# A fused attention, routing and two-expert-layer kernel: where the last exponentials of a pair are summed, and the order of the work in the first pair and around the first expert

## The chip, the cores and the metric

The kernel runs on one core of one Trainium2 chip. The metric is the device time of one execution in microseconds; for the kernel before three executions were timed. PE is the matrix engine (TensorE), PEld its weight loads, DVE the vector engine, ACT the scalar engine, POOL the GpSimd engine, and SP (SPq is its queue) the engine that only issues DMA transfers here.

## The reference

Three layers follow each other. B = 2, H = 8, S = 768, D = 64; there are 1536 tokens of width 512.

```python
# 1: attention, masked to the keys of the query's own cluster (16 clusters per head)
q_assign = argmax(q_n . c_n);  k_assign = argmax(k_n . c_n)
scores = where(q_assign == k_assign, q k^T / 8, -1e9)
scores = scores - max(scores, axis=-1)
attn = exp(scores);  attn = attn / (sum(attn, -1) + 1e-9);  x = attn @ v
# 2: mixture of 8 experts, noisy gate, two experts a token
noisy = x @ w_gate + log1p(exp(x @ w_noise)) * noise
for e in range(8): out[tokens of e] += weight * (relu(x @ w1[e]) @ w2[e])
# 3: soft mixture of 8 experts with 4 slots each: softmax over tokens, relu layer, softmax over slots
```

## The kernel before

Attention works on 8 pairs of heads (p = 0 to 7). Keys are split in 6 blocks of 128 and queries in two halves (qh), so a pair has 12 steps t: `score` (line 366) makes 128 keys by 2 x 384 query scores in PSUM with four matmuls and ACT takes their exponential into a buffer `pt` (line 378, five buffers in turn); `av` (line 381) multiplies it with the values; `add` (line 394) sums the exponentials for the denominators. For p = 6 and 7 the blocks kc = 0, 1, 2 are summed on POOL (line 408, then 411, tile `psa`) and kc = 3, 4, 5 on DVE (tile `psb`); only the last block of (7, 1) is not added. `den` (line 430) sums over keys with eight matmuls for each head pair of each part (line 440), and `xout` (line 449) turns and scales the result.

The maximum of a row is taken first, over scores made once more at lower precision: `munit` (line 320) is one such unit, two or one matmuls and one DVE reduction (lines 334, 339, 344), nine for each (p, qh). `mfin` (line 346) puts the nine together and writes the negative maxima as row 96 of the query operand (for p = 0 through PE and ACT, lines 355 and 357). The scores of a half can't start before that row is there. Cluster masks are extra rows 64 to 95 of the operands: `sims`, `masks`, `first_rows` (pair 0) and `mask_rows` (later pairs, by DMA). `hk`, `hq`, `ak`, `aq` are the high parts of q and k, written by ACT, and `akl`, `aql` the low parts, by POOL (lines 306, 316).

The order is written out by hand and every engine runs its instructions in that order. After a set-up the loop at line 1659 goes through 98 steps, two at a time: units of `pre`, two scores, `mid`, the `av` and the `add` of the two steps before, then `post`. Global step s is pair s // 12, t = s % 12. I call two steps a group by its first step: group 84 holds the first two scores of pair 7. `gap` puts the gate's small instructions (lines 539 to 745) between.

The first expert layer (`MoE1`) starts after group 96, in steps s of one eighth of an expert. Its weights come by DMA (`load_w`, line 934, four buffers `wr`), are split in a high part by ACT and a low part by DVE (`split_hi` line 944, `split_lo` line 951, about 0.5 MB each), and go into `first(s)` (line 1046) and `second(s)` (line 1087). Before, six splits (0 to 5) stand in pair 7 (SP, line 57), and split s + 3 stands in step s from s = 3 on. At s = 8 SP reads the order of the later experts (`load_perm`) and issues `load_x(2)`, the gathered tokens of the third job; `load_w(13)` stands ahead of it.

Of the kernel before, what the change touches and what calls it, by code (L numbers as in the profile page):

```python
# [17 lines left out]
NP = B * H // 2  # L18
# [38 lines left out]
SP = 1, 2, 3, 4, 6, 8  # L57
# [3 lines left out]
B7 = 8  # L61
B2 = 1
TF = (0, 0), (0, 1)
ORD, U1, Z1, R1, Z0 = (1, 1, 1, 0, 1, 0, 1, 1), 3, 8, 4, 2
M2S = 14, 15, 16, 18, 20
# [20 lines left out]
class Attention:  # L86
# [6 lines left out]
    def __init__(self, tc, g, qk, q2, k2, v2, cent, wgn):  # L93
# [16 lines left out]
        self.u1 = 0  # L110
# [7 lines left out]
    def load(self, p):  # L118
        nc, g = self.nc, self.g
        q, k = g.raw[p % 2][:, 0:2, :], g.raw[p % 2][:, 2:4, :]  # L120
        nc.sync.dma_start(q, self.q2[p])
        nc.sync.dma_start(k, self.k2[p])
        self.raws[p] = (q, k)
# [9 lines left out]
    def setup(self):  # L133
# [11 lines left out]
        self.identr = self.AQ[1][:, 1, 1, 256:]  # L145
# [46 lines left out]
    def fixed(self):  # L192

        nc = self.nc
        nc.gpsimd.memset(f32(self.BK[0])[96:97], 1.0)
        nc.gpsimd.memset(f32(self.BK[1])[64:96], 0.0)
        nc.gpsimd.memset(f32(self.BK[1])[96:97], 1.0)

    def setup2(self):
# [5 lines left out]
        for hh in range(2):  # L205
            nc.sync.dma_start(self.iw[64 * hh:64 * hh + 64, :, 128 + 16 * hh:144 + 16 * hh],
                              self.wgn.rearrange("(a h p) n -> h p a n", h=2, p=64)[hh])
        self.sel = g.xp.tile([128, 2, 32], F32, name="sel")
        nc.gpsimd.memset(self.sel, 0.0)
        for hh in range(2):  # L210
            nc.gpsimd.memset(self.sel[:, hh, hh:hh + 1], 1.0)

# [31 lines left out]
    def first_rows(self):  # L244
# [18 lines left out]
        self.hk(0, 1)  # L263
# [56 lines left out]
    def munit(self, p, qh, u):  # L320
# [6 lines left out]
        if p or u % 2:  # L327
# [66 lines left out]
    def add(self, p, t):  # L394
# [5 lines left out]
        if kc == first or (p, t) == (NP - 1, 11):  # L400
            return
# [28 lines left out]
    def den(self, p, qh):  # L430
# [3 lines left out]
        if (p, 6 * qh + 5) in self.ptile:  # L434
            parts.append(self.ptile.pop((p, 6 * qh + 5)))
# [32 lines left out]
class Dispatch:  # L468
# [24 lines left out]
    def setup(self):  # L493
# [4 lines left out]
        nc.sync.dma_start(self.noise, self.noise_in)  # L498
# [12 lines left out]
        dv.tensor_scalar(self.lim[:, 1:, :NREG], self.lim[:, 1:, :NREG], float(LATE - RCAP), None, op0=OP.add)  # L511
# [3 lines left out]
        for n in range(0, NSL // 128, 4):  # L515
            m = min(4, NSL // 128 - n)
            io(self.zm[:, n:n + m, 3], [[128, m]], TRASH, 1)
        nc.sync.dma_start(g.xg[:, DM:].rearrange("(n p) d -> p n d", p=128), self.zm)
        dv.tensor_scalar(self.tri, g.jp, 0.0, None, op0=OP.is_gt)
        dv.memset(self.onesb, 1.0)  # L520
        dv.memset(self.cum[:, 0, :], 0.0)
        nc.gpsimd.tensor_copy(g.x[:, :, DM + 3], self.tok)
# [932 lines left out]
def body(tc, qk, q2, k2, v2, cent, wgn, noise, w12, phi, v12, out):  # L1455
    nc = tc.nc
    with ExitStack() as ctx:
# [45 lines left out]
        g.stk = M1.WR.rearrange("p a b -> p (a b)")[:, :2 * S].rearrange("p (a s) -> p a s", a=2)  # L1503
        A = Attention(tc, g, qk, q2, k2, v2, cent, wgn)
        Dp = Dispatch(tc, g, noise)

        A.setup()
        A.sims(0)
        A.busy(B7)
        A.hk(0, 0)  # L1510
        A.hq(0, 0)
# [8 lines left out]
        for i in range(2):  # L1520
            A.ak(0, i)
            A.akl(0, i)
            if i == 0:
                A.fixed()
        for i in range(2):
            A.aq(0, i)
            A.aql(0, i)
        for u in range(A.MU):
# [6 lines left out]
        todo1 = [lambda i=i: A.masks(1, i) for i in range(5)] + [lambda: A.mask_rows(1)]  # L1535
        for i in ORD:
            if i:
                todo1.pop(0)()
            else:
                A.munit(0, 1, A.u1)  # L1540
                A.u1 += 1
        EARLY = A.u1
        A.setup2()
        Dp.setup()
# [6 lines left out]
        for p in range(-1, NP):  # L1551
            s0 = 12 * p
            if p >= 0 and p + 1 < NP:
# [7 lines left out]
                a, z = (2, 7) if p else (U1, Z1)  # L1561
                for u in range(A.MU):
                    at(pre, s0 + a + 2 * u // 3, A.munit, n, 0, u)
                    at(pre, s0 + 8 + 2 * u // 3, A.munit, n, 1, u)
                at(post, s0 + z, A.mfin, n, 0)
                at(post, s0 + 13, A.mfin, n, 1)
# [274 lines left out]
```

## Time and profile before

| | us |
|---|---|
| median of the 3 runs | 648.34 |
| lowest and highest run | 648.06, 650.31 |
| the profiled execution | 641.98 |
| its span (first to last instruction) | 640.2 |
| PE busy in the span | 612.9 (96%) |
| DVE, ACT, POOL busy | 404.2, 311.2, 278.5 |

The profile lists for every engine when it ran and what ended each wait. A row of the timeline gives start, duration, engine, source line, operation, the tile written and the tiles read, how many were merged (xN), and in brackets the idle time before it and what ended it. A row of the stretches gives the length, the busy time of PE, PEld, DVE, ACT and POOL with their instruction counts, the granted PE clock (1.00 is 2.4 GHz, 0.50 is 1.2 GHz), the DMA share and GB/s.

### The profile page before, as it was taken

To read this page: it belongs to the slowest core of one execution; us is meant where nothing else is said; L and a number is where in the kernel's file an instruction comes from. 1 tells how busy PE (TensorE), PEld (TensorE's weight loads), DVE (VectorE), ACT (ScalarE), POOL (GpSimd) and SP (SyncE) were. 2 spreads that over 40 slices of the span, in tenths; PEclk is the share of its full clock that TensorE was granted. 3 is DMA by queue.
4 is the path that set the end of the run, shared out by engine and by line. 5 is a ranking of instruction groups with operands and counts; after the bars stand their busy time and mean duration, and the time that the engine had idled before them with its cause. 6 is when DMAs were issued, how large, how long until landed. Compare 5 with 4: busy or idle time off the path is not lost. (4 is left out here: it accounts for less than half of the span.)

```text
span 640.2 us, 11046 instructions
## 1 busy us (share of the span) xinstructions
PE 612.9 (96%) x3973; PEld 472.5 (74%) x3973; DVE 404.2 (63%) x856; ACT 311.2 (49%) x444; POOL 278.5 (43%) x268
## 2 busy tenths in 40 slices
PE   7899999999999997998999999999999999988996
PEld 5566666666766666886888888888888988876444
DVE  6777888877777688766555445555454557646633
ACT  5576575756767462345344343443534446533002
POOL 3899675858678850733034132332412403120100
PEclk9599999999999898999999999999999999999999
DMA  8392846728344364696926739889795949978995
GB/s 317 81 269 65 305 133 200 247 66 308 118 136 157 150 176 139 221 227 234 193 98 146 198 138 236 323 253 294 255 298 194 194 161 313 313 259 288 429 384 198
DMA packets 62890, 139.47 MB, mean 218 GB/s; under 512 B 15280, under 2 KB 30832, under 8 KB 60784
## 3 DMA queue, kind: packets, MB, share of 16 engines
q1 hardware_dynamic: 56944, 125.31, 58.8%
q0 software_dynamic: 5888, 13.42, 9.6%
q8 instruction: 32, 0.52, 0.4%
q14 instruction: 26, 0.21, 0.1%
HBM read 108.18 MB, written 28.42 MB: 213 GB/s over the span
## 5 line engine op out<-in xcount | busy, mean ns | idle before, releaser
L1087 PE MATMUL py<-ring,H 128*128 128x512 f32 (+1 forms) x686 | 172.4, 395 | 0.7 <-DVE H L1055 0.7
L951 DVE TENSOR_TENSOR ring<-wr,ring 128x1024 fp32r<-128x1024 f32 (+1 forms) x77 | 97.0, 1261 | 105.1 <-ACT ring L944 102.9
L1087 PEld LDWEIGHTS py<-ring,H 128*128 128x128 f32 (+1 forms) x686 | 123.8, 184 | 27.4 <-DVE H L1055 1.7
L944 ACT ACTIVATE ring<-wr 128x1024 fp32r<-128x1024 f32 x77 | 81.5, 1059 | 93.2 <-PE py L1087 80.7
L378 ACT ACTIVATE pt<-psc 128x768 f32<-128x768 f32 x96 | 77.5, 811 | 74.8 <-PE psc L375 66.8
L1095 POOL DMA_INDIRECT x2acc<-y,mdi x31 | 50.4, 1625 | 103.6 <-ACT y L1120 97.7
L391 PE MATMUL pav<-pt,vt 128*64 128x384 f32 x384 | 73.3, 504 | 0.0
L339 DVE TENSOR_REDUCE mp<-pmx 128x1 f32<-128x512 f32 x96 | 63.0, 675 | 14.2 <-PE pmx L334 13.2
L1052 ACT ACTIVATE H<-ph 128x256 fp32r<-128x256 f32 (+7 forms) x80 | 36.6, 458 | 68.1 <-PE ph L1046 62.0
L1046 PE MATMUL ph<-XS1a,ring 128*128 128x240 f32 (+3 forms) x288 | 67.8, 326 | 0.0
L411 POOL TENSOR_TENSOR psa<-psa,pt 128x768 f32<-128x768 f32 x32 | 61.1, 1910 | 5.4 <-ACT pt L378 3.3
L1046 PE MATMUL ph<-XS0a,ring 128*128 128x432 f32 (+3 forms) x252 | 63.2, 333 | 0.1
L1055 DVE SCALAR_TENSOR_TENSOR H<-ph,H 128x384 fp32r<-128x384 f32 (+2 forms) x120 | 43.4, 389 | 18.9 <-ACT H L1052 18.0
L1046 PEld LDWEIGHTS ph<-XS1a,ring 128*128 128x128 f32 x288 | 47.8, 188 | 3.6 <-DVE ring L951 0.2
L1046 PE MATMUL ph<-XS0b,ring 128*128 128x256 f32 (+3 forms) x192 | 46.7, 316 | 2.6 <-ACT ring L944 2.0
L1046 PE MATMUL ph<-XS1b,ring 128*128 128x240 f32 (+3 forms) x192 | 46.1, 314 | 0.8 <-DVE ring L951 0.8
L1046 PEld LDWEIGHTS ph<-XS0a,ring 128*128 128x128 f32 x252 | 43.6, 191 | 2.7 <-issue 0.6
L1014 POOL TENSOR_TENSOR XS0b<-xr,XS0a 128x512 fp32r<-128x512 f32 (+1 forms) x9 | 16.8, 1871 | 64.7 <-ACT XS0a L1008 64.7
L391 PEld LDWEIGHTS pav<-pt,vt 128*64 128x64 f32 x384 | 23.5, 136 | 24.9 <-issue 19.4
L749 POOL DMA_INDIRECT xg<-x,idx x24 | 26.3, 1096 | 25.4 <-DVE inv L682 19.0
L344 DVE TENSOR_REDUCE mp<-pmx 128x2 f32<-128x512 f32 x48 | 33.0, 690 | 6.1 <-PE pmx L334 6.0
L334 PE MATMUL pmx<-even 96*128 96x512 f32 (+1 forms) x96 | 33.9, 411 | 1.6 <-ACT even L258 0.8
(364 smaller groups left out, 1003.2 us busy)
## 6 DMA issues: line engine op xcount, KB each, us to landing
wr<-in_w SPq DMA_DIRECT2D x80, 512.0 KB
v<-in_v SPq DMA_DIRECT2D x9, 2048.0 KB
xg<-xr SPq DMA_DIRECT2D x14, 512.0 KB
wr<-in_qk SPq DMA_DIRECT2D x8, 768.0 KB
early<-in_q SPq DMA_DIRECT2D x8, 768.0 KB
early<-in_k SPq DMA_DIRECT2D x8, 768.0 KB
x2acc<-xr SPq DMA_DIRECT2D x8, 512.0 KB
vt<-in_v SPq DMA_DIRECT2D x8, 384.0 KB
```

The source lines that it names most:

```text
L334: nc.tensor.matmul(o, self.BQ[i][:96, qh, hh, 128 * c:128 * c + 128], self.BK[i][:96, hh, ks], start=True, stop=True)
L339: nc.vector.tensor_reduce(mp[:, 0, col:col + 1], ps, axis=AX.X, op=OP.max)
L378: nc.scalar.activation(pt, ps[:, :, :384], AF.Exp, scale=SCALE)
L391: nc.tensor.matmul(self.avp[p, qh][64 * hh:64 * hh + 64, :384], self.vt[p][:, hh, kc, :], pt[:, hh, :], start=(kc == 0), stop=(kc == 5))
L411: eng.tensor_tensor(s, s, pt.pop((p, t)), op=OP.add)
L944: self.nc.scalar.activation(self.ring[s][0], self.wr[s], AF.Copy)
L951: nc.vector.tensor_tensor(lo[:, :n], wr[:, :n], f32(hi)[:, :n], op=OP.subtract)
L1046: nc.tensor.matmul(ph[:, :u], a[:, 128 * c:128 * c + 128], x[:, c, :u], start=(c == 0 and i == 0), stop=(c == 3 and i == 2))
L1052: nc.scalar.activation(HH[:, :u], ph[:, :u], AF.Relu)
L1055: nc.vector.scalar_tensor_tensor(o[:, :b - a], ph[:, a:b], 0.0, f32(HH)[:, a:b], op0=OP.max, op1=OP.subtract)
L1087: nc.tensor.matmul(o, x, y, start=(f == 0 and i == 0), stop=(f == NF - 1 and i == 2))
L1095: st = nc.gpsimd.indirect_dma_start(out=out, out_offset=bass.IndirectOffsetOnAxis(ap=di, axis=0), in_=y, in_offset=None, compute_op=OP.add)
```

## The change

Each exponential that DIRECT names (the last block of (6,0), (6,1), (7,0), and the last three of (7,1)) goes into `den` as a part of its own and is not added on DVE. `den` and `xout` of pair 6 come one step earlier. Pair 7 has five splits, spread two steps apart; splits 5 to 8 stand in the expert steps 0 to 3, each with the load of the weight four further on; from step 8 on `load_w` stands behind `load_perm` and `load_x(2)`. In the set-up k is loaded ahead of q for pair 0, `hk(0, 1)` comes right behind `hk(0, 0)`, the gate's constants on POOL come first, and the three memsets of `fixed` come between and behind POOL's low parts. `lim`, `tri`, `onesb`, `cum` and the loads of the noise and of `zm` move to step 31. In group 0 the two scores stand ahead of `masks(1, 3)`, `masks(1, 4)`, `mask_rows(1)` and of three units; the units of pair 1 start in group 4. Three dummy matmuls go (B7).

```diff
-SP = 1, 2, 3, 4, 6, 8
+SP = 1, 3, 5, 7, 9
+DIRECT = {(6, 0): 1, (6, 1): 1, (7, 0): 1, (7, 1): 3}
-B7 = 8
+B7 = 5
+EARLY = 2
-ORD, U1, Z1, R1, Z0 = (1, 1, 1, 0, 1, 0, 1, 1), 3, 8, 4, 2
-M2S = 14, 15, 16, 18, 20
+FIRST = 3 * (4,) + 4 * (6,) + 4 * (8,) + 4 * (10,) + 3 * (12,)
+R1, Z0 = 3, 2
+M2S = 15, 15, 17, 18, 20
...
     def load(self, p):
-        nc.sync.dma_start(q, self.q2[p])
-        nc.sync.dma_start(k, self.k2[p])
+        for t, src in ((k, self.k2), (q, self.q2)) if p == 0 else ((q, self.q2), (k, self.k2)):
+            nc.sync.dma_start(t, src[p])
...
-    def fixed(self):
+    def fixed(self, i):
-        nc.gpsimd.memset(f32(self.BK[0])[96:97], 1.0)
-        nc.gpsimd.memset(f32(self.BK[1])[64:96], 0.0)
-        nc.gpsimd.memset(f32(self.BK[1])[96:97], 1.0)
+        if i:
+            nc.gpsimd.memset(f32(self.BK[1])[64:96], 0.0)
+        nc.gpsimd.memset(f32(self.BK[i])[96:97], 1.0)
...
     def first_rows(self):
-        self.hk(0, 1)
         krows(1)
...
     def munit(self, p, qh, u):
-        if p or u % 2:
+        if p or qh or u % 2:
             ps = g.psum.tile([128, 512], F32, tag="mx", bufs=2, name="pmx")
...
     def add(self, p, t):
-        if kc == first or (p, t) == (NP - 1, 11):
+        if kc == first or kc >= 6 - DIRECT.get((p, qh), 0):
             return
...
     def den(self, p, qh):
-        if (p, 6 * qh + 5) in self.ptile:
-            parts.append(self.ptile.pop((p, 6 * qh + 5)))
+        parts += [self.ptile.pop((p, 6 * qh + kc)) for kc in range(6) if (p, 6 * qh + kc) in self.ptile]
...
         A.setup()
+        A.setup2()
+        Dp.setup()
         A.sims(0)
         A.busy(B7)
         A.hk(0, 0)
+        A.hk(0, 1)
...
         for i in range(2):
             A.ak(0, i)
             A.akl(0, i)
-            if i == 0:
-                A.fixed()
         for i in range(2):
             A.aq(0, i)
+            if i == 0:
+                A.fixed(0)
             A.aql(0, i)
+        A.fixed(1)
...
-        A.setup2()
-        Dp.setup()
+        for i in range(3):
+            A.masks(1, i)
+        for u in range(EARLY):
+            A.munit(0, 1, u)
...
+                for fn in (0, 0, lambda: A.masks(1, 3), lambda: A.masks(1, 4), lambda: A.mask_rows(1)):
+                    at(pre, 0, fn or (lambda: None))
                 for u in range(EARLY, A.MU):
-                    at(pre, (u - EARLY) * 2 // R1, A.munit, 0, 1, u)
+                    at(pre, 0 if u < EARLY + R1 else 2, A.munit, 0, 1, u)
...
-                    for s, fn in zip(LT[qh] if p == NP - 1 else (8, 10, 12), (A.total, A.den, A.xout)):
+                    for s, fn in zip(LT[qh] if p == NP - 1 else (8, 9, 11) if p == NP - 2 else (8, 10, 12), (A.total, A.den, A.xout)):
...
+        at(post, 1, A.load_g)
+        at(post, 31, Dp.setup2)
...
         for s in range(ns):
             j, f = M1.steps[s]
-            if 4 + len(SP) <= s + 5 < ns:
-                M1.load_w(s + 5)
             if s == LX:
                 while todo:
                     gap(1000, 1000)
                 M1.load_perm()
                 M1.load_x(2)
+            if 13 <= s + 5 < ns:
+                M1.load_w(s + 5)
...
-            if len(SP) <= q < ns:
+            if s < 4:
+                q = s + 5
+            if s < 4 or 9 <= q < ns:
                 M1.split_hi(q)
                 M1.split_lo(q)
+            if s < 4:
+                M1.load_w(q + 4)
```

## Rows read from the trace of the kernel before

**Rows 1.** The page: busy time of the engines; the costliest group of splits (busy, mean ns).
```profile
PE 612.9 (96%) x3973; PEld 472.5 (74%) x3973; DVE 404.2 (63%) x856; ACT 311.2 (49%) x444; POOL 278.5 (43%) x268
...
L951 DVE TENSOR_TENSOR ring<-wr,ring 128x1024 fp32r<-128x1024 f32 (+1 forms) x77 | 97.0, 1261 | 105.1 <-ACT ring L944 102.9
```

**Rows 2.** Stretches: length, busy of PE, PEld, DVE, ACT, POOL; clock, DMA share, GB/s.
```profile
120.00:140.00 20.00, 20.00 (x141) 14.21 (x141) 15.25 (x35) 11.15 (x16) 11.94 (x8) 1.00 0.56 183
...
20.00:30.00 10.00, 7.97 (x27) 5.07 (x27) 6.33 (x13) 4.64 (x7) 8.44 (x43) 0.50 0.31 98
...
6.00:8.00 2.00, 1.57 (x10) 0.49 (x11) 0.91 (x7) 0.00 (x0) 0.00 (x0) 1.00 1.02 427
...
30.00:32.00 2.00, 2.00 (x9) 1.96 (x8) 1.01 (x3) 0.53 (x1) 2.00 (x2) 0.64 0.71 44
...
212.00:214.00 2.00, 2.00 (x13) 1.82 (x13) 1.16 (x3) 0.98 (x2) 1.83 (x2) 0.91 0.35 136
...
248.00:250.00 2.00, 2.00 (x10) 2.00 (x10) 1.43 (x8) 0.00 (x0) 0.00 (x0) 0.52 0.01 4
```

**Rows 3.** Timeline, all engines, from the start to the second row of maxima.
```profile
9.08 0.56 DVE L231 TENSOR_TENSOR xr<-xr 128x384 bf16<-128x384 f32 x1
...
9.79 0.84 ACT L295 ACTIVATE even<-early 64x768 fp32r<-64x768 f32 x1 [4.72 <-DMA early<-in_k]
...
10.72 1.83 POOL L306 TENSOR_TENSOR even<-early,even 64x768 fp32r<-64x768 f32 x1 [8.79 <-ACT even L295]
...
18.81 3.90 POOL L316 TENSOR_TENSOR even<-early,even 64x768 fp32r<-64x768 f32 x2
...
19.66 0.80 ACT L357 ACTIVATE even<-pnm 1x768 fp32r<-1x768 f32 x1
19.66 1.38 DVE L231 TENSOR_TENSOR xr<-xr 128x384 bf16<-128x384 f32 x1
...
22.86 0.52 PE L373 MATMUL psc<-even 97*128 97x384 f32 x1
...
25.67 0.69 DVE L511 TENSOR_SCALAR lim<-lim 128x2 f32<-128x2 f32 x1 [2.30 <-POOL lim L510]
...
35.83 0.80 ACT L357 ACTIVATE even<-pnm 1x768 fp32r<-1x768 f32 x1 [0.96 <-PE pnm L355]
```

**Rows 4.** Timelines of DVE, POOL and PE, the end of attention and the first expert.
```profile
204.05 2.42 DVE L411 TENSOR_TENSOR psb<-psb,pt 128x768 f32<-128x768 f32 x1
...
235.03 0.96 DVE L411 TENSOR_TENSOR psb<-psb,pt 128x768 f32<-128x768 f32 x1
...
241.52 1.30 DVE L1001 STREAM_TRANSPOSE xr<-xr 128x512 f32<-128x512 f32 x2
...
257.94 0.42 DVE L1055 SCALAR_TENSOR_TENSOR H<-ph,H 128x256 fp32r<-128x256 f32 x1 [0.40 <-ACT H L1052]
...
228.39 1.85 POOL L411 TENSOR_TENSOR psa<-psa,pt 128x768 f32<-128x768 f32 x1
...
208.10 0.50 PE L334 MATMUL pmx<-oddb 96*128 96x256 f32 x2 [1.43 <-DVE mp L339]
...
236.04 0.54 PE L440 MATMUL pden<-psb,sel 128*32 128x96 f32 x16 [1.02 <-DVE psb L411]
...
246.29 0.74 PE L440 MATMUL pden<-psb,sel 128*32 128x96 f32 x16 [4.10 <-DVE psb L408]
...
258.94 0.19 PE L728 MATMUL prank<-xr,tri 128*128 128x24 bf16 x1 [0.46 <-DVE xr L682]
```

**Rows 5.** Timeline, SP, ACT and PE, expert steps 12 to 14: the weights' DMA and who waits.
```profile
284.37 1.96 SPq L940 DMA_DIRECT2D wr<-in_w  x2
...
290.88 1.06 ACT L944 ACTIVATE ring<-wr 128x1024 fp32r<-128x1024 f32 x1 [4.67 <-DMA wr<-in_w]
...
287.02 1.59 PE L1046 MATMUL ph<-XS0b,ring 128*128 128x256 f32 x12
...
291.99 0.50 PE L1046 MATMUL ph<-XS0b,ring 128*128 128x256 f32 x2 [1.99 <-ACT ring L944]
```

More of the change, by code (lines that the diff above doesn't have):

```diff
@@ L109, in __init__ @@
         self.ptile, self.stile, self.avp, self.ots, self.rds = {}, {}, {}, {}, {}
-        self.u1 = 0
     def busy(self, n):
@@ L143, in setup @@
         half = lambda n: g.place(n // 2).bitcast(BF16)
-        self.identr = self.AQ[1][:, 1, 1, 256:]
+        self.identr = g.turner
         nc.gpsimd.tensor_copy(self.identr, g.ident)
@@ L204, in setup2 @@
             nc.gpsimd.tensor_copy(self.iw[:, hp, :128], g.ident)
-        for hh in range(2):
-            nc.sync.dma_start(self.iw[64 * hh:64 * hh + 64, :, 128 + 16 * hh:144 + 16 * hh],
-                              self.wgn.rearrange("(a h p) n -> h p a n", h=2, p=64)[hh])
         self.sel = g.xp.tile([128, 2, 32], F32, name="sel")
@@ L211, in setup2, with load_g @@
             nc.gpsimd.memset(self.sel[:, hh, hh:hh + 1], 1.0)
+    def load_g(self):
+        for hh in range(2):
+            self.nc.sync.dma_start(self.iw[64 * hh:64 * hh + 64, :, 128 + 16 * hh:144 + 16 * hh],
+                                   self.wgn.rearrange("(a h p) n -> h p a n", h=2, p=64)[hh])
     def sims(self, p):
@@ L497, in setup @@
                                                      allow_small_or_imprecise_dtypes=True)
-        nc.sync.dma_start(self.noise, self.noise_in)
         io(self.iode, [[-1, E]], E, 0)
@@ L510, in setup @@
         nc.gpsimd.tensor_tensor(self.lim, self.base, self.capm[:, None, :].to_broadcast([128, B, E]), op=OP.add)
-        dv.tensor_scalar(self.lim[:, 1:, :NREG], self.lim[:, 1:, :NREG], float(LATE - RCAP), None, op0=OP.add)
         io(self.tok, [[128, NCK]], 0, 1)
@@ L517, in setup, with setup2 @@
             io(self.zm[:, n:n + m, 3], [[128, m]], TRASH, 1)
+        nc.gpsimd.tensor_copy(g.x[:, :, DM + 3], self.tok)
+    def setup2(self):
+        nc, g = self.nc, self.g
+        dv = nc.vector
+        nc.sync.dma_start(self.noise, self.noise_in)
         nc.sync.dma_start(g.xg[:, DM:].rearrange("(n p) d -> p n d", p=128), self.zm)
+        dv.tensor_scalar(self.lim[:, 1:, :NREG], self.lim[:, 1:, :NREG], float(LATE - RCAP), None, op0=OP.add)
         dv.tensor_scalar(self.tri, g.jp, 0.0, None, op0=OP.is_gt)
@@ L521, in setup @@
         dv.memset(self.cum[:, 0, :], 0.0)
-        nc.gpsimd.tensor_copy(g.x[:, :, DM + 3], self.tok)
     def fill(self, i):
@@ L1503, in body @@
         g.stk = M1.WR.rearrange("p a b -> p (a b)")[:, :2 * S].rearrange("p (a s) -> p a s", a=2)
+        g.turner = M1.XT[1][0][:, :128]
         A = Attention(tc, g, qk, q2, k2, v2, cent, wgn)
@@ L1534, in body @@
         turn()
[L1535 to L1542, printed above, removed]
-        A.setup2()
-        Dp.setup()
+        for i in range(3):
+            A.masks(1, i)
+        for u in range(EARLY):
+            A.munit(0, 1, u)
         pre, mid, post = {}, {}, {}
@@ L1560, in body @@
                     at(post, s0 + s, fn, n, i)
[L1561 to L1566, printed above, removed]
+                if p == 0:
+                    at(pre, 4, lambda: None)
+                for u in range(2 * A.MU):
+                    qh, v = divmod(u, A.MU)
+                    at(pre, s0 + (2, 8)[qh] + 2 * v // 3 if p else FIRST[u], A.munit, n, qh, v)
+                for qh in range(2):
+                    at(post, s0 + 7 + 6 * qh if p else (9, 13)[qh], A.mfin, n, qh)
             if p == 0:
+                for fn in (0, 0, lambda: A.masks(1, 3), lambda: A.masks(1, 4), lambda: A.mask_rows(1)):
+                    at(pre, 0, fn or (lambda: None))
                 for u in range(EARLY, A.MU):
-                    at(pre, (u - EARLY) * 2 // R1, A.munit, 0, 1, u)
+                    at(pre, 0 if u < EARLY + R1 else 2, A.munit, 0, 1, u)
                 at(post, Z0, A.mfin, 0, 1)
@@ L1583, in body @@
                 if p + 4 < NP:
-                    at(post, max(s0 + 15, 0), A.load_s, p + 4)
+                    at(post, max(s0 + 15, 3), A.load_s, p + 4)
         for n in range(2, NP):
```

## The prediction

> **What bounds the kernel now.** I read the page first: PE is busy for 612.9 us of a span of 640.2 [rows 1], so 27 us of waiting is all that a better order can take from PE, unless it also takes away slow time. Next the stretches: in the middle of attention PE is busy for all of its 20 us at full clock [rows 2], and nothing that is moved there pays. Two kinds of place are left. From 20 to 30 us PE is busy for 7.97 us of 10 and the granted clock is 0.50, that is 1.2 GHz [rows 2]: the first pair waits and is slow besides. And in the timelines of the end of attention PE stops for 1.43 us at 206.7, 1.02 at 235 and 4.10 at 242, each time for DVE [rows 4], and in the first expert for 1.99 us at 290, for a weight [rows 5]. The clock falls behind two of these: it is 0.91 over 212 to 214 and 0.52 over 248 to 250 [rows 2]. So the change is judged in three stages: the first pair, the end of attention, and expert steps 0 to 14.
>
> **The start.** Before, ACT begins `hk(0,0)` at 9.79 because k lands last [rows 3]. One of the two transfers is 786 KB; at 427 GB/s [rows 2] that is 1.8 us, so with k first `hk` runs from about 8.0 and POOL's L306 from 8.8, where it ran from 10.72 for 1.83 us [rows 3]. But DVE's L231, which all masks of pair 0 wait for, stands at 9.08. Alone it takes 0.56; beside POOL's L316 the same instruction took 1.38 [rows 3], as if it waited for POOL's instruction to end. So L231 would now wait until 10.6 and end at 11.1 instead of 9.64. I take 1.2 us later for the first masks and so for the first maxima (0, if POOL does not hold it, and 1.5). The constants on POOL now run beside DVE's set-up, from 2 to 6.5 us. Their bounds: nothing, or what L511 shows, 0.69 us for two elements beside a POOL memset [rows 3], some 0.5 too much, for each of nine steps, 4.5. I take 0, because POOL's single constants are short beside the memset of L511 and up to 1 us of delay disappears in L231's wait for L306. The Trainium skill, page "SBUF — State Buffer", section "Who interferes with whom", says that a DVE instruction with two SBUF inputs is shut out only by a GpSimd instruction that reads SBUF, and tensor_scalar in its two-port modes by any: by it L306 would hold L231, and of the set-up the four tensor_scalar steps alone could be held, 4 x 0.5 = 2.0 us at most instead of 4.5; L511 in the trace agrees.
>
> **The first pair.** Row 96 of the first half was written by L357 from 19.66 to 20.46; 1.2 later is 21.7. Score 0 began at 22.86 [rows 3], behind a wait for POOL's low parts and for the mask of pair 1. With the memsets behind `aql(0,0)` POOL is done with it by about 16, and the mask matmul now stands behind scores 0 and 1, so score 0 starts at 21.7: 1.2 us won. From there to the second L357 (35.83 [rows 3]): 2.03 us of idle lie in 20 to 30 [rows 2], of which about 0.5 lies behind score 0 and goes. The clock, at 0.64 over 30 to 32, came back at 31.4 [rows 2]; after the restart at 208.10 it came back by 212.4 (0.91 over 212 to 214), 4.3 us later [rows 2, 4]. If PE runs without a gap from 21.7 it comes back near 26; 5.4 us of half clock less is worth 2.7. Two units of pair 1 leave the stretch, 0.2 each. Sum 1.2 + 0.5 + 2.7 + 0.4 = 4.8. DVE must still take nine reductions and POOL its twelve 1.8 us additions and differences, which starts only 2 us earlier, so I take 4.0 us. The low end is 1.5: the clock comes back only after a pause of PE for DVE's third reduction. High end 5.2, without L231's wait. From group 4 on PE was full, so this gain stays.
>
> **Moved out of the start.** The noise, `zm` and four DVE steps (0.69 for L511 [rows 3], 1.6 together) now come at step 31, where DVE is busy 15.25 of 20 and PE 20.00 [rows 2]: cost 0 beside PE; 1.6 if DVE had no room. Three dummy matmuls of PE go where PE waits for L231 anyway: 0. `load_g` behind group 0 is needed by the first `xout` only: 0.
>
> **Direct denominators.** Each adds one part to `den`, 0.54 us for a part [rows 4]; there are four more, 2.0 us on PE at most. In return L411 at 204.05 goes, which took 2.42 us beside POOL, with PE's wait of 1.43 and the 4.3 us at half clock behind it (2.1) [rows 2, 4]; L411 at 235.03 goes with the wait of 1.02; and L408 in front of the wait of 4.10 goes [rows 4]. That would be 8.6 us. It is not all won, for what is late next is known: exponential 91 needs the buffer that POOL's L411 frees at 230.24 [rows 4], and POOL runs from 203.8 to there almost without a pause; it gets perhaps 1.5 faster, so PE can be at most some 2.6 us ahead there. Behind it DVE sets the pace: it reaches the transposes of the first tokens at 241.52 without a wait [rows 4]. Of its queue two L411 of 0.96 and one split of 1.26 [rows 1, 4] go, 3.2 us, and splits further apart meet POOL less often. I take the transposes 3.7 us earlier. From there the gate's chain on DVE leads to `second(0)`, and L408, about 0.9, goes from it: 4.5 us earlier in all. PE will then wait for the `ot` of ACT and for DVE's H where it waited for L408; these waits are inside the 4.5. Low end 2.5 (the tokens' DMA, issued when POOL's scatters have landed, gets no earlier), high end 5.4.
>
> **Splits 5 to 8 in steps 0 to 3.** Split 5 now stands between the gate's last exponential and `second(1)`'s H: ACT 1.06 [rows 5], then DVE 1.26 [rows 1], both in front of the H at 257.94 and of the gate steps that the rank matmul at 258.94 waits for; PE had already waited 0.46 for it [rows 4]. 1.06 + 1.26 less the 0.40 that DVE waited there: PE loses 2.0. Splits 6 to 8 come in front of nothing that PE needs within its 2.8 us a step: 0; if each cost as much, 6 more.
>
> **Weight 13 behind the tokens.** `load_x(2)` waits for the experts' order; the first weight behind it went at 284.37 and ACT had it at 290.88 [rows 5]: that was weight 14. Now it is weight 13 that stands there. `first(13)` ran at 287.02 and would start at 291.99, as `first(14)` did; the wait of 1.99 and 0.2 becomes one of 5. PE has one step less done at that time: 2.8 us lost. Bounds: -0.7 (a weight issued at 284.37 lands in 3 us) and 4.9 (the clock falls in a wait of 5 us as it did behind 4.10, 2.1 more).
>
> **Sum.** 4.0 + 4.5 - 2.0 - 2.8 = 3.7 us won. Against the profiled execution (span 640.2, 641.98 with what lies around it) that is 638.3; the median of the three runs is 6.4 us above the profiled one, and I take the same difference from it: 648.34 - 3.7 = 644.6.
>
> **The rivals.** (a) Weight 13 is not late, since the DMA engines take it beside the tokens; for it speaks that the tokens' pieces leave GB/s unused, against it weight 14 in the same place. Then 3.7 + 2.8 = 6.5 won: 641.8. (b) The clock takes the gain: PE pauses in group 0 and it comes back late (1.5 instead of 4.0), or it falls in the 5 us wait (2.1 lost): 1.2 to 1.6 won, 646.9. For it speaks that it fell behind 1.43 us of waiting [rows 2, 4]; against, that it did not behind the 1.99 at 290. (c) Slower: the splits in steps 0 to 3 come in series with the gate on DVE, each at the 2.0 us of split 5. It decides where DVE's work of a step, with H, gate steps and a split, exceeds PE's 2.8 us. Then 4.0 + 4.5 - 8.0 - 2.8 = -2.3, and with the clock falling in these pauses -4.4: 650.6 to 652.7. The single wait of 0.46 speaks against DVE being that full; its 28 gate steps in step 0 speak for it. (d) The direct parts save nothing because POOL's chain holds PE: 2.0 less, 646.6; I count it with (b).
>
> **How the numbers follow.** Forecast 0.40 (643 to 646.2), (a) 0.15, (b) with (d) 0.32, (c) 0.13. About 0.5% or 3.2 us is what a measurement of this kernel can tell from no change. Faster than 645.1: (a) and most of the forecast, 0.48. Slower than 651.6: the dear half of (c) and mishaps, 0.09. The rest, 0.43, is within. For 8 in 10 the range takes (a) and the cheap half of (c): 640.5 to 649.5.
>
> **What would show it.** Score 0 near 21.7, the second L357 near 31.8, clock back near 26; L231 over 1 us long at the start. No L411 of DVE from 200 us on, no PE wait at 206 or 235; a wait for `ot`, not for `psb`, at the last `den`. A PE wait of about 2.5 us in front of the rank matmul, and one near 5 us in front of `first(13)` for weight 13. It is wrong if that last one is missing, if the clock is low for long in group 2, or if `second(2)` to `second(5)` wait for H.

## The result and the profile after

The change made the kernel slower by half a per cent, 3.6 us between the medians, where it was forecast 3.7 us faster; the time is above the range (640.5 to 649.5) too.

| us | before | after |
|---|---|---|
| median (20 executions each) | 648.33 | 651.97 |
| lowest and highest | 643.72, 650.44 | 647.25, 656.21 |
| ratio, 95% interval | | 1.0052 [1.0032, 1.0072] |
| the profiled execution | 641.98 | 647.25 |
| its span | 640.2 | 645.4 |
| PE busy, DVE busy | 612.9, 404.2 | 612.1, 397.1 |

To see where the time went, both traces are cut at starts of PE instructions that stand in both: px(p, qh), the first matmul of `xout` (L459) for pair p and half qh, and `first(s)`. Lines of after are those of before plus 3 to 6 (its L411 is the L408 of before); `lim` and `tri` stand at 525 and 526. (What the recorded texts of the experiments call first(1) and first(3) are first(2) and first(4) here: first(0) and first(1) run as one.) The third column is a second trace of the same changed kernel, the fourth a second trace of the kernel before; both come with the experiments.

| stage, us | before | after | after again | before again | forecast |
|---|---|---|---|---|---|
| start to px(0,0) | 56.80 | 52.18 | 56.77 | 55.34 | 4.0 won |
| to px(1,1) | 39.77 | 39.76 | 39.72 | 39.81 | 0 |
| to px(2,0), with step 31 | 13.76 | 15.65 | 17.01 | 13.79 | 0 |
| to px(5,1) | 93.39 | 93.36 | 93.37 | 93.37 | 0 |
| to first(2), with second(0) | 50.37 | 48.55 | 46.79 | 51.56 | 4.5 won |
| to first(4), with split 5 | 6.43 | 8.31 | 8.28 | 6.16 | 2.0 lost |
| to first(8) | 11.25 | 13.74 | 11.24 | 17.53 | 0 |
| to first(13), with weight 13 | 15.25 | 18.57 | 18.55 | 15.26 | 2.8 lost |
| to first(16) | 13.49 | 13.52 | 12.57 | 13.62 | 0 |
| to the end | 339.67 | 341.78 | 340.44 | 339.17 | 0 |
| sum | 640.18 | 645.42 | 644.74 | 645.61 | 3.7 won |

Four things stand out. Step 31 costs 1.9 to 3.3 us. Weight 13 costs 3.3. The start is worth 4.6 in one execution and nothing in another. And the kernel before itself takes 7.2 us more between px(5,1) and first(8) in its second trace than in its first: 1.2 to first(2) and 6.3 from first(4), less 0.3 between.

**The start**, timeline of the kernel after (start, duration, engine, line, operation), then two stretches (length, busy of PE, PEld, DVE, ACT, POOL; clock, DMA share, GB/s):
```profile
4.98 0.80 DVE L176 TENSOR_SCALAR xr<-xr,cnn 128x64 f32<-128x64 f32 x1
...
9.02 1.77 DVE L235 TENSOR_TENSOR xr<-xr 128x384 bf16<-128x384 f32 x1
...
8.55 3.90 POOL L309 TENSOR_TENSOR even<-early,even 64x768 fp32r<-64x768 f32 x2 [1.85 <-ACT even L298]
...
21.50 0.41 PE L376 MATMUL psc<-even 97*128 97x384 f32 x1 [0.47 <-ACT even L360]
...
20.00:30.00 10.00, 8.98 (x58) 5.88 (x56) 8.77 (x17) 7.82 (x11) 4.71 (x4) 0.99 0.34 111
```
The mask step L235 ends with POOL's first difference, as it was forecast: 1.77 us where L231 took 0.56 [rows 3]. Score 0 starts at 21.50, forecast 21.7, and 20 to 30 us run at a clock of 0.99 instead of 0.50 [rows 2]. The second trace of the same kernel does not have that; the mask step in it, held for longer, and the same stretch:
```profile
8.93 2.07 DVE L235 TENSOR_TENSOR xr<-xr 128x384 bf16<-128x384 f32 x1
...
8.77 3.91 POOL L309 TENSOR_TENSOR even<-early,even 64x768 fp32r<-64x768 f32 x2 [2.09 <-ACT even L298]
...
20.00:30.00 10.00, 9.62 (x36) 6.42 (x36) 6.41 (x11) 4.88 (x7) 3.28 (x3) 0.50 0.28 96
```

**Step 31**, timeline of the kernel after:
```profile
94.10 1.71 DVE L525 TENSOR_SCALAR lim<-lim 128x2 f32<-128x2 f32 x1
95.72 0.21 DVE L526 TENSOR_SCALAR tri<-ident_i 128x128 bf16<-128x128 f32 x1
...
93.96 1.82 POOL L411 TENSOR_TENSOR psa<-pt 128x768 f32<-128x768 f32 x1
...
96.74 0.50 PE L337 MATMUL pmx<-oddb 96*128 96x256 f32 x2 [1.83 <-DVE mp L342]
```
A step of two elements per partition takes 1.71 us, until POOL's sum ends. DVE's next reduction is late by that, and PE waits 1.83 for the bank of the maxima that it frees. In the second trace PE waits 1.82 there, and the clock falls to 0.50 behind it, which makes 17.01 of the stage where the first has 15.65. Timeline of that trace and a stretch behind it:
```profile
101.28 0.56 PE L337 MATMUL pmx<-oddb 96*128 96x256 f32 x2 [1.82 <-DVE mp L342]
...
102.00:104.00 2.00, 2.00 (x8) 0.54 (x6) 2.00 (x2) 0.00 (x0) 1.92 (x2) 0.50 0.29 83
```

**The end of attention and the first expert**, timeline of the kernel after:
```profile
237.81 1.30 DVE L1007 STREAM_TRANSPOSE xr<-xr 128x512 f32<-128x512 f32 x2
...
242.62 1.08 PE L459 MATMUL px<-iw,ot 128*128 128x160 f32 x6 [1.83 <-ACT ot L424]
...
256.22 0.19 PE L734 MATMUL prank<-xr,tri 128*128 128x24 bf16 x1 [2.33 <-DVE xr L688]
...
283.93 1.65 SPq L946 DMA_DIRECT2D wr<-in_w  x3
...
289.02 1.06 ACT L950 ACTIVATE ring<-wr 128x1024 fp32r<-128x1024 f32 x1 [5.90 <-DMA wr<-in_w]
...
290.12 3.23 PE L1052 MATMUL ph<-XS0b,ring 128*128 128x256 f32 x12 [3.22 <-ACT ring L950]
...
280.00:300.00 20.00, 16.78 (x87) 14.60 (x86) 7.87 (x12) 7.56 (x11) 5.32 (x4) 0.83 0.79 219
```
The transposes come at 237.81, 3.7 us before 241.52 [rows 4]; but 2.8 of these were won ahead of px(5,1) (200.95 against 203.72), so the end of attention itself brings them forward by 0.9, and in the second trace by 2.7 (241.94 behind a px(5,1) at 206.87). PE waits for `ot` and no longer for `psb`; the rank matmul waits 2.33 instead of 0.46 for the gate, behind split 5. `first(13)` waits 3.22 for weight 13 and then takes 3.23 us, where it took 1.59 [rows 5]: it runs at 1.2 GHz.

### The profile page after: what moved, and what is told of

It reads as the page before. It is cut to its first block, busy times and chain, and to the rows that moved or that the text cites. A ratio compares the mean times of both kernels' runs of the same rounds, so it can differ in the third digit from the quotient of the medians.

```text
span 645.4 us, 11153 instructions
## 1 busy us (share of the span) xinstructions
PE 612.1 (95%) x4031; PEld 472.2 (73%) x4031; DVE 397.1 (62%) x852; ACT 310.7 (48%) x444; POOL 278.8 (43%) x268
## 5 line engine op out<-in xcount | busy, mean ns | idle before, releaser
L1052 PE MATMUL ph<-XS0b,ring 128*128 128x256 f32 (+3 forms) x192 | 48.2, 327 | 3.6 <-ACT ring L950 3.2
L1052 PEld LDWEIGHTS ph<-XS0b,ring 128*128 128x128 f32 x192 | 32.3, 201 | 6.2 <-ACT ring L950 3.6
```

The costliest lines, as they stand in the source:

```text
L1052: nc.tensor.matmul(ph[:, :u], a[:, 128 * c:128 * c + 128], x[:, c, :u], start=(c == 0 and i == 0), stop=(c == 3 and i == 2))
```

## The experiments

Ratios are to the kernel before on the same chip; as recorded they differ from the ratio of the medians by up to 0.3%. They carry from chip to chip only roughly: the kernel after has 1.0052 in the result and 1.0115 on another chip, which is 4 us. A price that is a difference of two ratios, taken on different chips or at different times, is no surer than that, so the stages of the traces decide where they can. "Lost to the clock" is the span times one less the mean granted clock, averaged over the executions behind the ratio; it tells how much of a difference is slow PE time. For the kernel after it is 15.2 us; for the kernel before 14.2 on the chip of the first four experiments.

### Weight 13 ahead of the tokens

Undoes one move only.
```diff
+            if 13 <= s + 5 < ns:
+                M1.load_w(s + 5)
             if s == LX:
...
                 M1.load_x(2)
-            if 13 <= s + 5 < ns:
-                M1.load_w(s + 5)
```


> The changed kernel with one order put back: in expert step 8 the load of weight 13 is issued ahead of the third expert's tokens. Theory: the place in SP's queue is the whole cause of the wait of 3.22 us in front of first(13) and of the half clock behind it; first(13) then starts without a wait near 286.7 and weight 14 takes over the wait, near 2 us as in the kernel before; 4 us less than the changed kernel, so about 648 us, level with before. Rival: the load is slow because the DMA engines share it with the tokens whatever the order; then first(13) still waits 2 us or more and the time stays at 651 to 652. In both, everything ahead of 280 us is the changed kernel's own: if the results of PE at 206, 223 and 262 us come late again, that belongs to the program; if they don't, it was that one execution.

Measured: 646.38 against 648.67, ratio 0.9968 [0.9944, 0.9992]. Timeline of this kernel, the mask step at the start, `first(13)` and `first(14)`:
```profile
8.87 0.56 DVE L235 TENSOR_TENSOR xr<-xr 128x384 bf16<-128x384 f32 x1
...
8.90 4.02 POOL L309 TENSOR_TENSOR even<-early,even 64x768 fp32r<-64x768 f32 x2 [2.21 <-ACT even L298]
...
285.88 1.59 PE L1052 MATMUL ph<-XS0b,ring 128*128 128x256 f32 x12
...
289.18 0.50 PE L1052 MATMUL ph<-XS0b,ring 128*128 128x256 f32 x2 [0.32 <-ACT ring L950]
```
Both waits are nearly gone, that of weight 14 too, for which the recorded text wanted near 2 us. The stage takes 15.20 us instead of 18.57, the one behind it 11.79 instead of 13.52. In all traces it is 15.2 to 15.3 with weight 13 ahead of the tokens (10 traces) and 18.5 to 20.0 behind them (7). From a ratio of 1.0052 to 0.9968 is 5.4 us; the time lost to the clock falls from 15.2 to 10.5, so 4.7 of the 5.4 are slow PE time. Not all of it need be weight 13's: at the start, where the program is that of the kernel after, DVE came to the mask step 0.03 us ahead of POOL in this execution and was not held, and px(0,0) came at 50.85 instead of 52.18. Weight 13 was late as forecast, and the clock fell in its wait, as the second half of rival (b) said.

### Step 31 without `lim`

`lim` goes back to the set-up, now on POOL.
```diff
-        dv.tensor_scalar(self.lim[:, 1:, :NREG], self.lim[:, 1:, :NREG], float(LATE - RCAP), None, op0=OP.add)
+        nc.gpsimd.tensor_scalar(self.lim[:, 1:, :NREG], ..., float(LATE - RCAP), None, op0=OP.add)   # in setup
```


> The changed kernel with the one-column addition on lim done by POOL in the set-up instead of by DVE at step 31. Theory: DVE stood 1.71 us in lim behind POOL's sum of exponentials, which held PE for 1.83 us and cost 1.9 of the 4.6 us won at the start; without it the gain stays 4.6 to px at 203.7, PE has no wait near 96.7, and the time is 1.9 us less, 650.1. Rival 1: the four instructions at step 31 take DVE's room whatever lim does (0.7 us more work): the wait stays at 1 us or more. Rival 2: the gain is there at 200 us but POOL's and DVE's chain at the end of attention takes it back, 651.5 or more.

Measured: 648.7 against 648.67, ratio 1.0009 [0.9979, 1.0040]. Timeline of this kernel at step 31:
```profile
94.94 1.77 DVE L526 TENSOR_SCALAR tri<-ident_i 128x128 bf16<-128x128 f32 x1
...
94.80 1.82 POOL L411 TENSOR_TENSOR psa<-pt 128x768 f32<-128x768 f32 x1
...
97.51 0.50 PE L337 MATMUL pmx<-oddb 96*128 96x256 f32 x2 [1.76 <-DVE mp L342]
```
The wait only moved: `tri`, 0.21 us in the kernel after, now takes 1.77. It isn't the operand but the place: whichever tensor_scalar comes first there stands behind POOL's sum. So this run didn't mend step 31, and its 2.8 us against after are no price of it.

### Splits back, direct denominators back

Two undo one part each: the splits and loads of weights 4 to 13 as before; and DIRECT reduced to what the kernel before did.
```diff
-SP = 1, 3, 5, 7, 9
+SP = 1, 2, 3, 4, 6, 8
...
-            if s < 4 or 9 <= q < ns:
+            if len(SP) <= q < ns:
```


> The changed kernel with the splits and loads of weights 4 to 13 where the kernel before has them. Theory: the wait in front of the rank matmul goes from 2.33 to about 0.5 and first(13) has no wait: 1.9 + 4.0 = 5.9 us less than the changed kernel, 646.1. Rival 1: splits 5 to 8 in steps 0 to 3 also cause the late H in steps 4 to 7 (second(4) waits 0.75, second(5) 1.22): then 2.5 more goes, 643.6. Rival 2: the gate's chain on DVE paces steps 0 to 2 whatever the splits do: only weight 13's share is won, 648.

```diff
-DIRECT = {(6, 0): 1, (6, 1): 1, (7, 0): 1, (7, 1): 3}
+DIRECT = {(7, 1): 1}
...
-        ... else (8, 9, 11) if p == NP - 2 else (8, 10, 12)
+        ... else (8, 10, 12)
```


> The changed kernel without the direct denominators of pair 6 and of the first half of pair 7, with one direct part in the last half and den and xout of pair 6 at the old steps. Theory A: the direct parts win what the changed trace shows for this stage, 1.8 us up to first(0); without them PE's waits of 1.43 at 206, 1.02 at 235 and 4.10 at 242 are back and the time is 653.8. Theory B, as forecast: they are worth 4.5 us and something else took the rest; then 656.5. Rival: the earlier den of pair 6 is itself what makes PE's results late at 206 and 223; then the time is that of the changed kernel or less, 650 to 652, with no wait of DVE for psc there.

Measured: 647.83, ratio 0.9967 [0.9940, 0.9994]; and 648.97, ratio 0.9991 [0.9958, 1.0023]; both against 648.67. The first is no better than weight 13 alone. The second is a surprise: without the direct denominators the kernel is not slower than the kernel after, but rather faster. In both traces ACT or DVE start on some results of PE late, without a cause among the waits that the profile names, which led to the next runs.

### The kernel before again, and the kernel after without its scatters

> The kernel before, unchanged, in one more profiled execution beside the others on this chip. Theory: the late arrival of PE's results (up to 3 us after the matmul's recorded end, in all five profiles of changed kernels) belongs to the order of the changed program; here none of some 650 results comes more than 0.3 us late, as in the first profile of this kernel. Rival: it belongs to the chip or to the execution; then late results show here as well, near 206 to 229 and 258 to 272 us.

```diff
     def scatter(self, ...):
+        return
```


> The changed kernel without the gate's scatters of the tokens (POOL's indirect DMAs from 203 us on are left out, so the experts get empty rows); all else stands. Theory: PE's late results in 206 to 225 and 258 to 270 us come from POOL's chain of scatters, since every late group lies inside such a chain; then none of PE's results is late by more than 0.3 us here, DVE's first reduction behind den(6,0) follows at once, and second(4) and second(5) don't wait for H. Rival: they come from PE's own stream; then the same 2.5 and 3.0 us stand behind den(6,0) and first(5).

Measured, one execution each: the kernel before has a span of 645.6 in this trace, 5.4 more than in the first (647.39 against a median of 648.75); the kernel after without scatters takes 646.35. Timeline of the kernel before again, `first(4)`, the second layer's matmuls behind, and the activation of the result of `first(4)`:
```profile
260.03 1.53 PE L1046 MATMUL ph<-XS0a,more 128*128 128x256 f32 x12
...
266.86 2.18 PE L1087 MATMUL py<-more,H 128*128 128x512 f32 x6 [2.48 <-issue]
...
266.42 0.38 ACT L1052 ACTIVATE H<-ph 128x256 fp32r<-128x256 f32 x1 [7.74 <-remote]
```
PE ends the first row at 261.56, and ACT, idle for 7.74 us, starts on the result at 266.42, 4.9 us later. The same is to be seen in the kernel after, at 206 us, where POOL's scatters run:
```profile
206.36 0.51 PE L442 MATMUL pden<-pt,sel 128*32 128x96 f32 x16
...
209.45 0.28 DVE L445 STREAM_TRANSPOSE dt<-pden 128x96 f32<-128x96 f32 x1 [4.42 <-PE psc L378]
209.62 1.51 ACT L381 ACTIVATE pt<-psc 128x768 f32<-128x768 f32 x2 [4.79 <-PE psc L378]
...
206.36 1.02 POOL L755 DMA_INDIRECT xg<-x,idx  x1 [0.16 <-issue]
207.68 0.98 POOL L755 DMA_INDIRECT xg<-x,idx  x1 [0.30 <-issue]
```
and not in the kernel without scatters, at the same `den`:
```profile
211.97 0.51 PE L442 MATMUL pden<-pt,sel 128*32 128x96 f32 x16
...
212.55 0.28 DVE L445 STREAM_TRANSPOSE dt<-pden 128x96 f32<-128x96 f32 x1 [1.91 <-PE pden L442]
```
DVE is at the result 0.07 us behind PE's end here, 2.58 in the kernel after. I counted results of PE that DVE or ACT, idle, took up more than 0.3 us after PE's recorded end: 0 of 655 in the first trace of before, 18 in its second, 12 in after, 10 to 17 in the six experiments with scatters on these two chips, 0 without scatters. All lie between 205 and 276 us, while POOL issues scatters or just behind them. That points to the scatters, though on one trace without them. They don't suffice, as the first trace of before shows and the next chip will; and while POOL's 31 later indirect DMAs run, which add the experts' rows, nothing comes late. What is late is PE's signal, the update of its semaphore, which the trace records apart from the matmul's end and mostly 0.01 us behind it. In the kernel after, the updates for ends at 206.87, 207.30, 208.00, 208.24 and 208.94 all stand between 209.42 and 209.61, while PE went on with its next matmuls.

What goes with it is seen from first(4) to first(8): 11.2 to 11.8 us in the six traces in which no result is late by over 0.44 us, 13.7 to 20.5 in the other eleven (17.4 to 20.5 with the old splits, 13.7 to 19.4 with the new ones).

### Only the start, and the start with the direct denominators

Both take `lim` out of step 31 and undo the splits and loads; the first undoes the direct denominators too.

> Of the change only the start and the first pair are kept (with the noise, zm and the small constants at step 31, and lim done by POOL in the set-up); direct denominators, splits, loads and the steps of pair 6 are those of the kernel before. Theory: 4.6 us are won up to px of pair 2 as in the changed kernel and nothing behind that place loses them: 643.7 to 644.5, ratio about 0.993. Rival 1: the end of attention is paced by POOL and DVE and takes the gain back: score 96 moves by less than 2 us and the time stays above 646.5. Rival 2: the late results of PE come with the start's edits; then they show in this trace too, and the time is 646 or more.

> As the kernel that keeps only the start, and with the direct denominators and the earlier den of pair 6 as well. Theory A (as forecast): the direct parts take the transposes 3.7 us and second(0) 4.5 us forward; with nothing behind that loses it, 4.5 us less than the start alone, 639.5. Theory B (the changed trace): PE's results come late behind den(6,0), which leaves 1.8 us: 642. Rival: the direct parts cost more than they save, as the kernel without them suggests (0.9991 of before where the changed kernel stood at 1.0052): this one is 1 to 4 us slower than the start alone.

Measured, against 648.75: 646.88, ratio 0.9983 [0.9954, 1.0011]; 646.5, ratio 0.9975 [0.9952, 0.9999]. The direct denominators make no difference that can be told in time here (0.4 us). Both traces have late results. The stage to first(2) takes 51.63 us without and 48.32 with the direct parts, so they do win 3.3 there; from first(4) to first(8) it is 17.38 and 19.98, which gives 2.6 of it back.

### A chip without late results: after again, and three mended kernels

On this chip the traces of the four kernels have 1, 1, 0 and 1 late results, none over 0.44 us, and the kernel before takes 639.15, where it took 648.3 to 649.7 on the others. This is the place to price the parts. The first is the kernel after unchanged; the others have weight 13 first and both `lim` and `tri` on POOL in the set-up; the third without the direct denominators, the fourth with the old splits and loads.
```diff
-        dv.tensor_scalar(self.tri, g.jp, 0.0, None, op0=OP.is_gt)
+        nc.gpsimd.tensor_scalar(self.tri, g.jp, 0.0, None, op0=OP.is_gt)   # in setup, beside lim
```


> The changed kernel, unchanged, beside the variants on this chip. Theory: its loss is weight 13: the single undoings put it 5 us of 3.6 + 2.1 down to that, so this one is 3 to 4 us slower than before again (ratio 1.004 to 1.007), with PE waiting 3 us or more in front of first(13) and half the clock behind it. Rival: the first measurement of it was unlucky, and with late results of PE in both kernels they are level: ratio 0.997 to 1.001.

> The changed kernel with two places mended: weight 13 loaded ahead of the tokens, and both one-off scalar instructions of DVE at step 31 (lim, tri) done by POOL in the set-up. Theory: DVE's first scalar instruction behind POOL's sum at step 31 stands 1.7 us whichever it is, so with none there the stretch from px(3,0) to px(4,0) takes 13.8 us as before and not 15.6, and first(13) has no wait: 5 + 1.8 us less than the changed kernel, about 645, ratio 0.994. Rival: another instruction of DVE takes the wait at step 31 (15.6 again), and the time is that of the kernel with weight 13 alone mended, 0.997.

> The same with two places mended, but without the direct denominators and with den and xout of pair 6 at the old steps. Theory A: between px(5,1) and px(7,1) the direct parts save 2.8 us (41.7 against 44.5 in the traces so far), and 2 of it reach first(8): this kernel is 2 us slower than the one with them, 647. Theory B: the scatters' chain on POOL sets the time of steps 3 to 7 and takes the saving back: within 0.7 us of it.

> The same with two places mended, but with the splits and loads of weights 4 to 13 where the kernel before has them. Theory A: from px(5,1) to first(8) this takes 74.7 us instead of 71, since ACT and DVE split weights in steps 3 to 7, where they wait for PE's late results; this kernel is 3 us slower than the one with early splits, 648. Theory B, as forecast: splits 6 to 8 lie in front of nothing that PE needs and only split 5's 1.9 us count, in favour of this kernel: 1 to 2 us faster, 643.5.

(The stage that the second text calls px(3,0) to px(4,0) is px(1,1) to px(2,0).)

| | median | ratio to 639.15 | lost to the clock | px(1,1) to px(2,0) | px(5,1) to first(2) | to first(4) | first(8) to first(13) |
|---|---|---|---|---|---|---|---|
| after again | 646.51 | 1.0115 [1.0073, 1.0158] | 14.0 | 17.01 | 46.79 | 8.28 | 18.55 |
| two mended | 636.7 | 0.9965 [0.9941, 0.9989] | 7.2 | 13.78 | 46.80 | 9.36 | 15.20 |
| no direct | 637.03 | 0.9975 [0.9949, 1.0002] | 6.7 | 13.76 | 47.84 | 8.29 | 15.21 |
| old splits | 634.94 | 0.9922 [0.9891, 0.9953] | 5.4 | 14.36 | 46.17 | 6.47 | 15.24 |

(Before on this chip: 10.5 lost to the clock.) The two mends together win 9.8 us on the same chip, and turn 1.0115 into 0.9965. The two traces are 11.1 apart and say where: start 5.7, step 31 3.2, weight 13 3.4 with 0.5 behind it, less 1.6 between first(2) and first(8). The start in the mended kernel:
```profile
4.97 0.26 DVE L176 TENSOR_SCALAR xr<-xr,cnn 128x64 f32<-128x64 f32 x1
...
8.54 0.56 DVE L235 TENSOR_TENSOR xr<-xr 128x384 bf16<-128x384 f32 x1
...
8.59 4.01 POOL L309 TENSOR_TENSOR even<-early,even 64x768 fp32r<-64x768 f32 x2 [0.96 <-ACT even L298]
```
L176 takes 0.26 instead of 0.80 (POOL's long memset stands 0.9 us later now), DVE reaches L235 0.05 us before POOL reaches L309, and L235 takes 0.56 instead of 1.77 or 2.07. The Trainium skill, page "SBUF — State Buffer", section "Who interferes with whom", has the rule that the prediction used at the start and not at step 31 (of the two, the one that issues first has the shared ports for its whole length). The trace agrees with it at L235, `lim` and `tri` (1.71 to 2.07 behind POOL's instruction; free, 0.56 for L235 and 0.21 for `tri`).

The price of split 5 is seen in the rank matmul. Timeline of the mended kernel and a stretch behind it:
```profile
251.46 0.19 PE L734 MATMUL prank<-xr,tri 128*128 128x24 bf16 x1 [2.31 <-DVE xr L688]
...
253.00:255.00 2.00, 2.00 (x9) 1.72 (x8) 1.93 (x11) 0.00 (x0) 1.70 (x2) 0.50 0.95 368
```
and with the old splits:
```profile
250.98 0.19 PE L734 MATMUL prank<-xr,tri 128*128 128x24 bf16 x1 [0.51 <-DVE xr L688]
```
2.31 less 0.51 is the 1.8 us of the gate behind a split, and in the mended kernel the clock falls to 0.50 behind it besides (9.36 instead of 6.47 for the stage). In neither trace of the kernel after does it fall there, behind 2.33 and 2.31 us.

### Step 31 alone, another order of the start, and all of it

The first moves `lim` and `tri` to POOL and leaves weight 13 late; the second only lets POOL make the other half of k first, so that L235 is not held:
```diff
-            A.akl(0, i)
+            A.akl(0, 1 - i)
```
The third has that order, `lim` and `tri` on POOL, the old splits and loads, and the direct denominators.

> The changed kernel with lim and tri done by POOL in the set-up and nothing else; weight 13 stays late. Theory: step 31's wait of 1.8 us (and the half clock that followed it in one execution, 1.4 more) goes, and the start's mask step on DVE comes just ahead of POOL's difference, since DVE's set-up is not held: 2 to 5 us less than the changed kernel, with first(13) still waiting 3 us: ratio to before 1.000 to 1.004 (the changed kernel 1.005 and 1.0115). Rival: nearly all of the 10 us is weight 13's, then 1.004 or more.

> The changed kernel with one order changed: POOL takes the difference of k's second half first, which waits for ACT's second copy and so can't start before 9.2 us, behind DVE's mask step at 9.0. Theory: the mask step takes 0.56 us instead of 1.77 to 2.1, the first maxima come 1.2 us earlier, PE pauses less, the clock is at half for less than 7 us between 10 and 56 us, and px(0,0) runs before 51.5 instead of 52.2 to 56.8: 2 to 4 us less than the changed kernel, 1.001 to 1.004 of before. Rival: the clock in the first pair has nothing to do with that step; then 10 us or more at half clock can show here too.

> All mends together: the start with POOL's two differences in the other order, lim and tri in POOL's set-up, the direct denominators, and the splits and loads of weights 4 to 13 as in the kernel before. Theory: it wins what the start (3 to 5 us) and the direct denominators (1 us) win, and nothing is lost: ratio 0.990 to 0.994 to before, px(0,0) before 51.5, no wait of PE near 96, no wait over 2.5 us in front of first(13). Rival: the other order moves POOL's chain of the first pair later, which holds score 0 or 1; then 0.995 or more.

Measured, against 649.68: 647.4, ratio 0.9983 [0.9958, 1.0008]; 654.17, ratio 1.0097 [1.0057, 1.0137]; 644.07, ratio 0.9928 [0.9897, 0.9958]. The first puts `lim` and `tri` at 4.5 us in time (from 1.0052), and step 31 takes 13.77 in its trace; the time lost to the clock fell from 15.2 to 10.5 there too. The second is a miss in time, as the recorded text wanted 1.001 to 1.004, though what it wanted of the start is in its trace: L235 takes 0.56, 6.8 us are at half clock between 10 and 56, px(0,0) comes at 51.48. That trace is long for other places: 17.05 at step 31 with the clock falling, and 19.41 from first(4) to first(8) with late results, where the second trace of the kernel after takes 11.24. Its time is therefore no verdict on the start.

The start can be read from all fifteen traces of kernels that have it, with the small differences told above. Where L235 is free (0.56, eight traces), px(0,0) comes at 50.5 to 52.3 us, with 3.4 to 6.8 us at half clock between 10 and 56. Where POOL holds it (1.77 to 2.16, seven traces), px(0,0) comes at 52.2 to 56.8, with 6.8 to 20.5. The kernel after can fall on either side: it was held in both of its traces, and not held in that of the kernel with weight 13 first, which has the same start. The third and "old splits" are the best kernels, 0.7 to 0.8% below the kernel before on either chip.

## Why the prediction was wrong

Two terms of the sum failed: step 31, put at 0, measured 1.9 to 3.3 us; and the start, put at 4.0, in which the hold of the mask step was priced at its own 1.2 us and not at the clock behind it, won 0.0 and 4.6 in the two traces of the kernel after.

Against the first trace of before, the second trace of after, in which no result is late by over 0.44 us either, is 4.56 us longer, where 3.7 less were forecast. The 8.3 us between them are the start 4.0, step 31 3.3, the end of attention 0.9 and weight 13 0.5; split 5 and the rest give back 0.4.

- **Step 31: the step that failed by a rule at hand.** The prediction put it at 0, from DVE's share of busy time (15.25 of 20 us [rows 2]), and its upper bound was 1.6. A share says that there is room somewhere, not that an instruction can start where it is put. The price was in [rows 3]: L511 took 0.69 us for two elements beside POOL. That was weighed for the start, where POOL's steps are short, and not for step 31, where they take 1.82. It measured 1.9 where the clock held behind the wait and 3.3 where it fell: over all traces the stage takes 15.6 to 15.7 us (six) or 17.0 to 17.1 (four) with `lim` or `tri` there, and 13.8 (one of five: 14.4) with both on POOL.
- **The start: order right, the price of the hold wrong.** Score 0 came at 21.50 (21.7), L235 took 1.77 (1.2 more than alone, forecast 1.2 more). But the clock came back at about 20 us, ahead of score 0, where the prediction had it at 26, behind it. So the 4.6 of the first trace is in part luck; the second won 0.03. Half-clock time between 10 and 56 us is 17.1 and 13.7 us in the two traces of before, and 6.8 and 20.5 in the two of after. With L235 free the start was won in all eight traces, 4.5 to 6.3 us against the first trace of before, 3.1 to 4.8 against the second. Rival (b) had the late clock, but from a pause in group 0; its 1.5 us was still too much, and 0.32 too little for it together with (d). Why the clock comes back early in some of the held executions is open.
- **The end of attention: right in mechanism, smaller in size.** No L411 (of before) on DVE, no PE wait for `psb`. In the first trace a wait of 1.83 stands at 210.78 even so, behind late results; in the second there is a new one of 1.65 for `pt` at 234.78. The transposes come 0.9 and 2.7 us earlier counted from px(5,1), forecast 3.7; that the first trace has 3.7 from the span's start is a coincidence. To first(2) it won 3.6 in the second trace, forecast 4.5; 1.8 in the first, where results are late. It is not additive: of the 3.6, spread splits without direct denominators win 2.5 (47.84 for the stage against 50.37), direct denominators without spread splits 4.2 (46.17), and in time the direct ones are worth 0.3 us (637.03 and 636.7). Why the kernel after without them was 4 us faster on the first chip (ratio 0.9991 against 1.0052, 11.2 us lost to the clock against 15.2) stays open; it is no more than the ratio of the kernel after itself differs between chips.
- **Split 5: right.** 1.85 to 1.88 lost, forecast 2.0. Rival (c), splits in series, did not come: first(4) to first(8) takes 11.24 in the second trace, 11.25 before.
- **Weight 13: mechanism right, size missed.** The wait is 3.22, not 5, but the clock falls in it and `first(13)` takes twice its time. 2.8 was forecast, 3.3 is in the traces of the kernel after. In time it is not settled: 5.4 by the kernel that has it mended alone, but 1.2 between the kernel with step 31 mended alone and the one with both (0.9983 and 0.9965), and neither pair was measured side by side.
- **The base.** The prediction took the 6.4 us between the median and the profiled execution as a constant. Behind it stands, as far as the runs show, a difference between the two: late results of PE. The first trace of before has none, and its 641.98 lies in the range of the one chip without them (636.0 to 642.7) and below every timed execution on the chip of the result (643.72). Before's second trace, which has them, is 7.2 us longer in the stages where they lie, more than the forecast difference, and what the change was to win there was measured on an execution without them. That the timed executions before had them is argued from their times, not shown. The profile held no row of it; the 6.4 us in themselves were the sign that the trace might not show the timed execution.

## What to carry to other kernels

Don't cost a moved vector instruction by the busy share of its engine; look up what POOL runs at that very place, since a step of 0.2 us standing behind a POOL instruction costs what is left of that, and then what PE waits for next. Price a new PE wait twice, with the clock falling behind it and without, since the same wait did both here, and count a gain that consists of clock as one that may not come. When two instructions of DVE and POOL come to their places within some tenths of a microsecond of each other, price both orders. When the profiled execution and the median lie 1% apart, find out what they don't share before the sum is made on one of them.

## What the runs showed of the hardware

- While POOL's scatters run, DVE and ACT can get PE's results up to 4.9 us after PE's recorded end (0 late in the one trace without scatters, 10 to 18 in every trace with them but the first of the kernel before and those of one chip). The updates of PE's semaphore come late and several at once (five within 0.2 us at 209.5), while PE goes on. The kernel before takes 639.15 on that one chip and 648.3 to 649.7 on the others. No run shows the mechanism, nor that the whole 9 us have this cause; the 7.2 of before's second trace do lie in those stages.
- The length of a PE wait alone did not tell whether the clock fell to 1.2 GHz behind it. It fell in or behind all seven waits of 3.1 to 4.6 us in front of `first(13)`; behind 2.31 to 2.33 at the rank matmul in 3 of 10 traces; behind 1.76 to 1.83 at step 31 in 4 of 10; behind 1.43 at 208.10 in the first trace of before [rows 4], and not behind the 1.43 at the same matmul in its second.
- Who comes first, DVE or POOL, decides 1.2 to 1.6 us of a DVE instruction, and 0.03 us of lead is enough (8.87 before 8.90: 0.56; 8.54 before 8.59: 0.56; 8.93 behind 8.77: 2.07; 9.02 behind 8.55: 1.77).
